# A fused mask-and-maximum, a moved load and a new instruction order in an attention-plus-experts kernel

## The chip, the cores and the metric

The kernel runs on one core of one Trainium2 chip. The core has a matmul engine (TensorE, PE in the profile), three engines for elementwise work (VectorE or DVE, ScalarE or ACT, GpSimd or POOL), and a sync engine (SyncE, SP) that here only issues DMAs. Each engine takes its instructions strictly in the order in which the program has them; semaphores hold an instruction until what it needs is there. The metric is the device time of one execution in microseconds (us), as the median over runs.

## The reference

Two layers follow each other. The first is attention inside clusters: for 4 batches and 8 heads, 768 positions and 64 dimensions per head, q and k are assigned to the nearest of 16 centres, and a position attends only to positions of its own cluster.

```python
q_assign = np.argmax(np.einsum('bhsd,hcd->bhsc', q_n, c_n), axis=-1)
k_assign = np.argmax(np.einsum('bhsd,hcd->bhsc', k_n, c_n), axis=-1)
mask = q_assign[:, :, :, None] == k_assign[:, :, None, :]
scores = np.where(mask, scale * np.matmul(q, k.transpose(0, 1, 3, 2)), -1000000000.0)
attn = softmax(scores);  x = np.matmul(attn, v)
```

The second is a mixture of 4 experts over x (4 x 768 x 512). A gate picks 2 experts per position; each expert is a causal attention head with its own wq, wk, wv (512 x 64) and wo (64 x 512):

```python
scores = scale * (q @ k.transpose(0, 2, 1))
scores = np.where(causal, -1000000000.0, scores)   # causal: key after query
a = softmax(scores);  ye = a @ v @ wo[e];  out += mask * w * ye
```

## The kernel before

The work is cut into 24 pairs. Pairs n = 0 to 15 are two attention heads of one batch each; n = 16 to 23 are two experts of one batch each (the "MoE" pairs, two per batch). A pair goes through these steps:

- *Operands* (`attention_operands`, `moe_operands`). For attention, q and k are loaded, transposed on TensorE (L531), multiplied with the normalised centres (L562), transposed again (L569), and VectorE finds the nearest centre (L574 to L582, L600). A one-hot row of the cluster, times a large number, is appended to q and k, so that a plain matmul gives masked scores. For MoE pairs q and k are projected (L764) and split into a high and a low part.
- *Row maxima* (`core`, from L955 on). L978 gives the scores of 128 queries against a block of keys in a PSUM bank, and VectorE's L988 reduces the bank to its maximum. In MoE pairs the block on the diagonal first gets the causal mask: L986 adds `tri` (128 x 128, 0 or -2^33) to the bank's last 128 columns. With 6 row blocks and 2 heads there are 12 such blocks per MoE pair, of width 128, 256, 384, 512, 320 and 384. L1004 (L1025 in pair 0) transposes the maxima, and a small DMA writes them as one more row of q.
- *Scores and values*. L1059 and L1060 compute the scores again, transposed; ScalarE's L1065 takes the exponential into a tile p; in MoE pairs GpSimd's L1070 clears what lies behind the diagonal; L1103 multiplies with v. The row sums are gathered in `acc` by additions on GpSimd or VectorE (L381, L382) and summed over partitions by L1127. The p tiles come from a ring: more tiles in the first layer, four (p0 to p3) in the MoE pairs, taken in turn, one per key block.
- *Normalising and output*. The sums travel through DRAM to be spread over partitions (`rb`). For MoE pairs VectorE or GpSimd multiplies `avu` by `rb`, one engine copies the high part (into `kt` or `xk`), and another subtraction gives the low part (`qt` or `xq`); `moe_out` (L1213) multiplies with wo, six blocks of 128 positions per batch, copies each from PSUM and stores it.

All of this is written as a list of operations. `plan.op` gives each a number, the engine, and for some an alternative engine. `SEQ`, a list of words, is the order in which they are issued: the word 3047p is operation 3047 on its alternative engine GpSimd (a: ScalarE, d: VectorE), a word without a letter the operation on its first engine. `SLOT` says which of its buffers each tile uses; `ps`, eight PSUM banks, is the longest. Because every engine keeps program order, SEQ fixes the order of all queues.

Constants and the centres' preparation (`centroid_op`) are not in SEQ; they are issued before it. SP loads the centres first (`dma(cf, ...)`), then k and q of pair 0. VectorE makes the constants, then squares the centres (L434), ScalarE takes the square root (L435) and loads the table of Exp by a dummy exponential (L436) that writes column 2 of the small tile `nr`; VectorE's L438 writes the same column. L443 gives the normalised centres, L449 transposes them and L453 copies them. `blk` (L425, L426, L444) and `tri` (L403) are made on the way. 37 `spin` operations (L1229) are matmuls that compute nothing and keep TensorE running in the head.

## Time and profile before

| | us |
|---|---|
| median of 3 runs | 701.16 (699.75 to 703.5) |
| the profiled execution | 701.95 |
| its span in the profile | 700.2 |
| TensorE busy | 680.8 (97%) |
| VectorE busy | 554.7 (79%) |
| ScalarE busy | 350.5 (50%) |
| GpSimd busy | 345.5 (49%) |

The span runs from the first to the last instruction of one execution; the time of that execution is 1.75 us longer. Busy is the time in which an engine executes; waiting for a semaphore is not counted. Mean durations of VectorE's operations are from start to end, and neighbours overlap a little. [...]

### The profile page before, as it was taken

To read this page: it belongs to the slowest core of one execution; us is meant where nothing else is said; L and a number is where in the kernel's file an instruction comes from. 1 tells how busy PE (TensorE), PEld (TensorE's weight loads), DVE (VectorE), ACT (ScalarE), POOL (GpSimd) and SP (SyncE) were. 2 spreads that over 40 slices of the span, in tenths; PEclk is the share of its full clock that TensorE was granted. 3 is DMA by queue.
4 is the path that set the end of the run, shared out by engine and by line. 5 is a ranking of instruction groups with operands and counts; after the bars stand their busy time and mean duration, and the time that the engine had idled before them with its cause. 6 is when DMAs were issued, how large, how long until landed. Compare 5 with 4: busy or idle time off the path is not lost.

```text
span 700.2 us, 13106 instructions
## 1 busy us (share of the span) xinstructions
PE 680.8 (97%) x4523; PEld 526.6 (75%) x4523; DVE 554.7 (79%) x1215; ACT 350.5 (50%) x863; POOL 345.5 (49%) x285
## 2 busy tenths in 40 slices
PE   8999999999999999999999999999999989999997
PEld 6778767767767767767767688879779877877876
DVE  6998798888899688989999977783887766467842
ACT  5447545645645735656746532543452344333653
POOL 4585647479656387575486516134322236242221
PEclk9999999999999999999999999999999999999999
DMA  8766759678665777687859744537455455554223
GB/s 231 197 149 157 182 130 239 145 163 236 174 157 147 190 188 196 164 199 180 172 136 252 172 115 123 152 117 172 107 130 129 100 138 153 124 131 122 87 85 121
DMA packets 78094, 109.64 MB, mean 157 GB/s; under 512 B 22432, under 2 KB 61516, under 8 KB 78028
## 3 DMA queue, kind: packets, MB, share of 16 engines
q1 hardware_dynamic: 78028, 108.81, 62.0%
q8 instruction: 36, 0.59, 0.4%
q14 instruction: 30, 0.25, 0.1%
HBM read 36.54 MB, written 12.91 MB: 71 GB/s over the span
## 4 chain that ended last, share of the span: by engine, by line
PE 81%; DVE 9%; DMA 4%; issue 2%; ACT 1%; POOL 1%; SPq 1%; DVEq 0%; ACTq 0%; POOLq 0%
PE ps L1103 20%; PE ps L978 12%; PE ps L1059 11%; PE ps L1060 11%; PE ps L764 9%; PE ps L1213 5%; PE ps L816 4%; DVE mx L988 3%; PE ps L531 2%; PE ps L1127 2%; DMA tq<-mr 1%; DVE oh L582 1%; PE ps L562 1%; SPq L369 1%; DMA vt<-x 1%
## 5 line engine op out<-in xcount | busy, mean ns | idle before, releaser
L988 DVE TENSOR_REDUCE mx<-ps 128x1 f32<-128x384 f32 (+1 forms) x448 | 223.1, 544 | 24.6 <-PE ps L978 22.5
L1059 PE MATMUL ps<-tq,tk 128*128 128x384 f32 (+2 forms) x528 | 178.4, 341 | 1.2 <-ACT p L1065 1.2
L1060 PE MATMUL ps<-tq,tk 97*128 97x384 f32 (+2 forms) x528 | 173.7, 332 | 1.1 <-DMA tq<-mr 1.0
L1065 ACT ACTIVATE p<-ps 128x384 f32<-128x384 f32 (+2 forms) x288 | 119.2, 461 | 64.8 <-PE ps L1060 39.3
L978 PE MATMUL ps<-tk,tq 80*128 80x384 f32 (+4 forms) x512 | 144.9, 353 | 4.2 <-ACT avu L376 1.9
L1059 PEld LDWEIGHTS ps<-tq,tk 128*128 128x128 f32 x528 | 100.3, 190 | 10.3 <-issue 3.8
L978 PEld LDWEIGHTS ps<-tk,tq 80*128 80x128 f32 x512 | 89.4, 190 | 21.7 <-issue 9.1
L1060 PEld LDWEIGHTS ps<-tq,tk 97*128 97x128 f32 x528 | 100.6, 191 | 2.7 <-DMA tq<-mr 1.8
L381 POOL TENSOR_TENSOR acc<-acc,p 128x768 f32<-128x768 f32 (+2 forms) x37 | 58.2, 1574 | 63.3 <-DVE acc L382 26.2
L1070 POOL TENSOR_SCALAR_AFFINE_SELECT p<-p 128x256 f32<-128x256 f32 x48 | 21.6, 466 | 76.2 <-ACT p L1065 57.1
L1065 ACT ACTIVATE xl<-ps 128x384 f32<-128x384 f32 x88 | 40.7, 497 | 26.3 <-PE ps L1060 26.0
L1103 PE MATMUL ps<-p,vt 128*64 128x384 f32 x288 | 50.7, 491 | 0.0
L986 DVE TENSOR_TENSOR ps<-ps,tri 128x128 f32<-128x128 f32 x96 | 28.1, 292 | 22.4 <-PE ps L978 22.3
L381 POOL TENSOR_TENSOR acc<-p,p 128x768 f32<-128x768 f32 (+1 forms) x11 | 19.3, 1754 | 50.6 <-ACT p L1065 34.0
L376 ACT ACTIVATE hi<-ps 128x384 fp32r<-128x384 f32 x38 | 18.6, 492 | 48.6 <-PE ps L764 38.9
L1103 PE MATMUL ps<-p,vm 128*64 128x384 f32 (+2 forms) x288 | 41.5, 423 | 0.0
L1065 ACT ACTIVATE xh<-ps 128x384 f32<-128x384 f32 x80 | 37.8, 498 | 5.2 <-PE ps L1060 4.7
L382 DVE TENSOR_TENSOR acc<-acc,p 128x768 f32<-128x768 f32 (+2 forms) x33 | 26.8, 811 | 14.8 <-POOL acc L381 7.7
L1103 PEld LDWEIGHTS ps<-p,vt 128*64 128x64 f32 x288 | 19.6, 136 | 23.7 <-issue 21.4
L1178 POOL TENSOR_TENSOR xt<-avu,rb 128x384 f32<-128x384 f32 x26 | 26.6, 1035 | 15.7 <-DMA rb<-rd 15.7
L988 DVE TENSOR_REDUCE M<-ps 128x1 f32<-128x512 f32 (+3 forms) x64 | 31.4, 491 | 2.2
L1103 PEld LDWEIGHTS ps<-p,vm 128*64 128x64 f32 x288 | 18.5, 136 | 19.1 <-issue 13.5
(271 smaller groups left out, 1447.6 us busy)
## 6 DMA issues: line engine op xcount, KB each, us to landing
tq<-hi SPq DMA_DIRECT2D x88, 192.0 KB
tk<-hi SPq DMA_DIRECT2D x60, 192.0 KB
tk<-lo SPq DMA_DIRECT2D x46, 192.0 KB
rb<-rd SPq DMA_DIRECT2D x46, 192.0 KB
tq<-lo SPq DMA_DIRECT2D x45, 192.0 KB
vt<-in_v_dram SPq DMA_DIRECT2D x16, 384.0 KB
x<-xt SPq DMA_DIRECT2D x16, 384.0 KB
tk<-hi SPq DMA_DIRECT2D x16, 384.0 KB
```

Of the source, the lines that this page charges most:

```text
L381: ways = [("pool", t_pool(n), lambda: POOL.tensor_tensor(dst(), a(), b(), op=fn)), ("dve", t_dve(n), lambda: DVE.tensor_tensor(dst(), a(), ...
L382: ("dve", t_dve(n), lambda: DVE.tensor_tensor(dst(), a(), b(), op=fn))]
L764: PE.matmul(m()[:, :HW], w_()[:, dc, es], x_[dc]()[:, c], start=(i == 0), stop=(i == 3 * DC - 1))
L816: PE.matmul(m()[:, :NV], x_[dc]()[:, ts], w_()[:, dc, :], start=(i == 0), stop=(i == 3 * DC - 1))
L978: PE.matmul(ps()[:, :w], Q[0:R, 0, h, c * 128:(c + 1) * 128], K[0:R, 0, h, i * w:(i + 1) * w], start=True, stop=True)
L986: DVE.tensor_tensor(e, e, tri, op=OP.add)
L988: DVE.tensor_reduce(to, ps()[:, :w], axis=AX.X, op=OP.max)
L1059: PE.matmul(p()[:, o_:HW], K[:, 1, h, ks], Q[:, 1, h, qs], start=True, stop=False)
L1060: PE.matmul(p()[:, o_:HW], K[0:R, 0, h, ks], Q[0:R, 0, h, qs], start=False, stop=True)
L1065: ACT.activation(pt()[:, h, o_:HW], p()[:, o_:HW], AF.Exp, scale=SC)
L1103: PE.matmul(av()[h * 64:(h + 1) * 64, o_:HW], d["vv"](h, kc), pt()[:, h, o_:HW], start=(kc == 0), stop=(kc == nk - 1), tile_position=(0, 6 ...
L1213: PE.matmul(m(), a_()[:, ts], w_()[:, ep, :], start=(ep == 0 and i == 0), stop=(ep == EP - 1 and i == 2))
```

## The change

- The centres' load is issued by ScalarE instead of SP.
- The dummy exponential writes a fifth column of `nr`. The small constants are set after the centres are normalised, and the four operations that make `blk` and the mask part of `tri` become one operation in SEQ (`go_blk`, operation 39; all later numbers go up by one). The first two L651 matmuls name it as needed.
- `tri` is 512 wide: 384 columns of 0, then the old 128. On the diagonal block one `tensor_tensor_reduce` adds it to the whole width and gives the maximum; it replaces L986 and L988 there. It writes the sum back to the bank.
- The exponentials of the last, 128 wide key block of a half (`o_ == 256`) go into the first 128 columns of the tile of the block before it, which uses only columns 128 to 383.
- The gate's scratch tiles use the buffers of two attention tiles.
- In the last batch the last of the six output blocks is made in two halves of 256 columns.
- SEQ and SLOT are new as a whole.

```diff
-    dma(cf, centroids.rearrange("h c d -> (h c) d"))
+    ACT.dma_start(cf, centroids.rearrange("h c d -> (h c) d"))
...
-        nr = sb.tile([128, 4], FT, name="nr")
+        nr = sb.tile([128, 5], FT, name="nr")
...
-        ACT.activation(nr[:, 2:3], nr[:, 0:1], AF.Exp, scale=0.0)
+        ACT.activation(nr[:, 4:5], nr[:, 0:1], AF.Exp, scale=0.0)
...
+        DVE.memset(tri[:, :384], 0.0)
...
+    def go_blk():
+        DVE.tensor_scalar(pi, pi, 67, None, op0=OP.bitwise_and)
+        DVE.tensor_scalar(di, di, 6, None, op0=OP.arith_shift_right)
+        DVE.tensor_tensor(blk, pi, di, op=OP.is_equal)
+        DVE.tensor_scalar(tri[:, 384:], jp, 0.0, -BIG, op0=OP.is_gt, op1=OP.mult)
     cbd_ready = centroid_op()
+    blk_ready = op("dve", 1.0, go_blk, base(0) + 10, at=4.9)
...
+                    to = mx()[:, h, cc, i:i + 1] if nb == 2 else tops(h)[:, cc:cc + 1]
                     if moe and i == nb - 1:
-                        e = ps()[:, w - 128:w]
-                        DVE.tensor_tensor(e, e, tri, op=OP.add)
-                    to = mx()[:, h, cc, i:i + 1] if nb == 2 else tops(h)[:, cc:cc + 1]
-                    DVE.tensor_reduce(to, ps()[:, :w], axis=AX.X, op=OP.max)
+                        DVE.tensor_tensor_reduce(ps()[:, :w], ps()[:, :w], tri[:, 512 - w:], 1.0, -3.0e38, OP.add, OP.max, to)
+                    else:
+                        DVE.tensor_reduce(to, ps()[:, :w], axis=AX.X, op=OP.max)
...
+                po = o_ - (256 if o_ == 256 else 0)
+                if po == o_:
+                    pt = p_tile(n)
...
-                        ACT.activation(pt()[:, h, o_:HW], p()[:, o_:HW], AF.Exp, scale=SC)
+                        ACT.activation(pt()[:, h, po:po + w], p()[:, o_:HW], AF.Exp, scale=SC)
...
+        blocks = [(c, 0, DM) for c in range(NC)]
+        if final:
+            blocks[-1:] = [(NC - 1, 0, DM // 2), (NC - 1, DM // 2, DM)]
```

Of SEQ, the two lines of before and of after that hold the operation 3047 (3048 after) and its neighbours:

```diff
-3526 3425 3215 3523 3178 3289 3288 3047p 3435 3297 3528 3304 3412 3216 3048 3312 3306 3433 3428 3120 3309 3307 3446
...
+3430 3428 3288 3048 3447 3523 3297 3306 3528 3524 3448 3527 3216 3179 3529 3289d 3217 3180 3441 3449 3298 3443 3433
```

There 3047 (after: 3048) is the subtraction xq = avu - xk of pair 17, 3215 and 3178 (3216 and 3179) are L1127 of pair 18, and 3288 (3289) is the first addition into `acc` of pair 19.

## Rows read from the trace of the kernel before

**Rows 1.** Windows by stage: length, busy PE, PEld, DVE, ACT, POOL; PEclk, DMA, GB/s.
```profile
28.00:400.00 372.00, 365.24 (x2435) 268.54 (x2434) 330.24 (x671) 215.28 (x513) 236.40 (x159) 1.00 0.73 177
400.00:680.00 280.00, 274.55 (x1810) 227.97 (x1810) 196.78 (x472) 115.34 (x312) 91.86 (x99) 0.99 0.49 126
```

**Rows 2.** Chain that ended last, first 40 us; columns: start, length (us), what.
```profile
0.81 0.39 SPq L369
...
1.26 0.42 SPq L369
...
1.73 4.70 DMA qt<-in_q_dram
...
10.29 0.57 DVE sm L574
...
22.84 2.65 DVE mx L988 x6
...
25.80 0.57 PE ps L1025 x3
```

**Rows 3.** Windows of 2 us at the longest stall; columns as rows 1.
```profile
560.00:562.00 2.00, 0.11 (x2) 0.04 (x1) 1.93 (x4) 0.58 (x2) 1.39 (x1) 1.00 0.98 252
562.00:564.00 2.00, 2.00 (x6) 1.84 (x7) 1.93 (x6) 1.66 (x5) 0.00 (x0) 0.51 0.64 143
564.00:566.00 2.00, 2.00 (x10) 1.62 (x9) 0.66 (x2) 0.49 (x3) 0.00 (x0) 0.64 0.01 3
```

**Rows 4.** Timeline there: start, us, engine, line, operation [idle before <- releaser].
```profile
558.34 1.28 POOL L381 TENSOR_TENSOR acc<-p,p 128x512 f32<-128x512 f32 x1 [6.57 <-PE ps L1127]
...
559.58 1.80 POOL L381 TENSOR_TENSOR xq<-avu,xk 128x768 fp32r<-128x768 f32 x1
...
561.42 0.49 ACT L376 ACTIVATE avu<-ps 128x384 f32<-128x384 f32 x1 [2.72 <-POOL xq L381]
...
561.96 0.65 PE L978 MATMUL ps<-tk,tq 80*128 80x384 f32 x1 [1.89 <-ACT avu L376]
```

**Rows 5.** Timeline of the head, VectorE and ScalarE; columns as in rows 4.
```profile
2.45 0.90 DVE L426 TENSOR_SCALAR acc<-acc 128x256 int32<-128x256 int32 x1
...
3.27 0.21 DVE L434 SCALAR_TENSOR_TENSOR avu<-rb 128x64 f32<-128x64 f32 x1
3.41 0.08 DVE L434 DVE_READ_ACCUMULATOR avu<-rb 128x1 f32 x1
...
3.74 1.28 ACT L436 ACT_TABLE_LOAD   x1
...
5.27 0.16 DVE L438 RECIPROCAL nr<-nr 128x1 f32<-128x1 f32 x1 [1.36 <-ACT nr L436]
...
6.44 0.42 DVE L444 TENSOR_TENSOR blk<-acc,acc 128x256 fp32r<-128x256 int32 x1
```

**Rows 6.** VectorE by form: xcount | busy us, mean ns | idle before.
```profile
L988 DVE TENSOR_REDUCE mx<-ps 128x1 f32<-128x384 f32 x416 | 208.4, 548 | 23.7 <-PE ps L978 22.1
L986 DVE TENSOR_TENSOR ps<-ps,tri 128x128 f32<-128x128 f32 x96 | 28.1, 292 | 22.4 <-PE ps L978 22.3
...
L582 DVE TENSOR_TENSOR oh<-ps,sm 128x384 bf16<-128x384 f32 x16 | 16.4, 1023 | 0.6
...
L575 DVE TENSOR_TENSOR ps<-ps,sm 128x384 f32<-128x384 f32 x16 | 9.1, 567 | 1.2
```

**Rows 7.** TensorE's waits from 400 to 680 us: total us, times, longest.
```profile
PE ps L1059 <- ACT p L1065: 1.2, 1, 1.2
...
PE ps L978 <- ACT p L1065: 0.7, 1, 0.7
```

**Rows 8.** Page, costliest groups: the causal mask on GpSimd; columns as in rows 6.
```profile
L1070 POOL TENSOR_SCALAR_AFFINE_SELECT p<-p 128x256 f32<-128x256 f32 x48 | 21.6, 466 | 76.2 <-ACT p L1065 57.1
```

**Rows 9.** Chain that ended last, its end; columns as in rows 2.
```profile
696.02 0.60 ACT xt L376
```

**Rows 10.** Busy time after the last matmul; columns as in rows 1.
```profile
696.00:698.00 2.00, 0.00 (x0) 0.00 (x0) 0.00 (x0) 0.60 (x1) 0.00 (x0) 1.00 1.01 375
```

## The prediction

> **What bounds the kernel now.** I read the page's busy shares and its chain first, then the busy time by stage, then the chain of the first 40 us, the timelines around the head and around the longest stall, and the tail. The busy shares (table above) put TensorE at 97%. By stage the reader sees that from 28 to 400 us TensorE is busy 365.24 of 372 us, and from 400 to 680 us 274.55 of 280 [rows 1]. So 6.76 + 5.45 = 12.2 us of waiting is left between head and tail, and the matmuls themselves, which the change does not make fewer, are the rest. VectorE is busy 330.24 of 372 us in the first of these stages but only 196.78 of 280 us in the second [rows 1]: work taken from it in the second stage is no work on the path.

> The head is another matter. Until 25.80 us, when the transposes of the first maxima run, the chain goes over the loads of k and q, q's transposes and the cluster matmuls, and then almost without a break over VectorE from 10.29 us on [rows 2]. The reader is to see there that q's load is late because of its place in SP's row of issues, and that from 10.29 us on VectorE's queue is what is long.

> [...] The timeline names the chain: a GpSimd sum into acc waited 6.57 us for L1127's matmuls, the subtraction xq<-avu,xk stood behind it on GpSimd and took 1.80 us, ScalarE's copy into avu waited for that, and L978 waited 1.89 us for the copy to free its PSUM bank [rows 4].

> **The change part by part.** Times are set against the profiled execution, 701.95 us (span 700.2), and moved by 701.95 - 701.16 = 0.79 us to the median at the end.

> *Loads.* The centres' load held SP's first place: SP issued it at 0.81 and k at 1.26 us [rows 2]. On ScalarE's queue it leaves k and q 0.45 us earlier. Bounds: 0, if the DMA engines and not the issue set q's landing, and 0.45; I take 0.45, since the row starts earlier with the same bytes behind it. On ScalarE the new issue is in front of everything; if the first table load stood in front of it, the centres would come 1.28 us later (the length of such a load [rows 5]), and that is covered by the next item.

> *Exp table.* L438 waits 1.36 us for the ScalarE instruction that loads the Exp table, because both write the same column of nr; with a column of its own that wait goes, and the normalised centres come 1.36 us sooner [rows 5]. What is late next is q: its second transpose and copy end after the centres. So little of the 1.36 is on the path. The centres' transposes leave the space between q's two transposes and go behind them; I count nothing for that.

> *Work put behind the centres.* The four index and mask operations (blk, tri) become one planned operation, which the new sequence puts on VectorE after q's second copy and before the first cluster maximum (L574). The longest of its parts takes 0.90 us, blk's comparison 0.42 [rows 5]; with the two others at 0.42 too, a bit over 2 us in all. They begin when q's second copy is done, by estimate at 7.4 us (q's landing at 6.43 - 0.45 = 5.98, then some 1.4 us for transposes and copy), and end near 9.5; a subtraction of 384 columns, priced as L575 at 0.57 [rows 6] less its overlap, follows. L574 could then start at 9.9 against 10.29 us: of the gain of 0.45 about 0.4 stays. Later on this queue the new sequence has one operation of 0.55 less before the first maxima and one of 0.4 more. Together the head gives -0.5 us. Bounds: -1.36 (the whole wait) and +0.5 (no earlier landing, and the planned operation late by its 0.9).

> *Mask and maximum in one.* 96 times (8 pairs, 2 heads, 6 row blocks) L986 (0.292) and L988 (0.548 at 384 columns) become one operation over the whole width [rows 6]. The trace has none of this kind. Nearest is L575, two operands and a PSUM result over 384 columns, 0.567 [rows 6], plus a read of the accumulator as behind L434, 0.08 [rows 5]: 0.65 against 0.84, so -0.19 x 96 = -18 us of VectorE. Bounds: -0.27 x 96 = -26 without the read, and with L582's 1.023 [rows 6] plus the read 1.10, +0.26 x 96 = +25 us. All of this lies in the stage where VectorE has 83.2 us free [rows 1], so I count 0 on the path; the upper end is a rival below.

> *Narrow exponentials share tiles.* Per MoE pair 7 instead of 9 tiles are taken from a ring of four. TensorE's two waits on exponentials in that stage are 1.2 and 0.7 us [rows 7], so 0 to -1.9; against it stands that GpSimd's mask of one key block and ScalarE's exponential of the next now write one tile, twice per pair, and if the one waited for the other each time, 16 x 0.466 = +7.5 [rows 8]. I take 0, since they write different columns.

> *Last block in halves.* The new sequence still ends on a whole block (c = 1), with one half before it. After the last matmul come the same copy of 0.60 [rows 9] and issue; the queue, which moves 375 GB/s from 696 to 698 us, has 128 KB less before it, at most -0.34 us [rows 10]. [...] I take -0.1, bounds -0.35 and +0.1.

> *The new sequence.* It leaves the amount of TensorE work alone. What I can read from it is the place of the chain at 560 us. Before, the subtraction was word 3047p, on GpSimd, right behind that waiting sum. Now it is word 3048, on VectorE, ahead of L1127's two operations, and the sum (3289d) is behind them. The chain cannot come back in that form. The stall goes: 1.89 us, and with it the slow clock, (1 - 0.51) x 2 + (1 - 0.64) x 2 = 1.70 us [rows 3, 4]. That is -3.6 us. The other 12.2 - 1.9 = 10.3 us of waits I leave as they are: the new sequence removes some and makes others. Against it speaks that between the transposes of a pair's maxima and its first scores there are now 8.3 TensorE entries on average instead of 11.1 (counted over 23 pairs in both sequences). Bounds: -5 (half of them go) and +3.6 (a stall with a slow clock somewhere else).

> Sum: 701.95 - 0.5 - 0.1 - 3.6 = 697.75, less 0.79: **697.0 us**.

> **The rivals.** *A stall of the same price comes up elsewhere:* only head and tail are won, 697.0 + 3.6 = 700.6. For it: the shorter cover above, and in-order queues with every engine. Against: only one wait in the stage from 28 to 680 us was long enough for the clock to fall.

> *The short waits go too:* half of 10.3, 697.0 - 5.1 = 691.9. For it: they are many and small, and VectorE gets time back. Against: the cover again.

> *The fused operation is slow, and the kernel gets slower.* At 1.10 us instead of 0.84, twelve of them add 0.26 x 12 = 3.1 us to each MoE pair on VectorE, right before the transposes of its maxima (L1004). VectorE is free only 30% of that stage [rows 1], so between none and 70% of it, 0 to 2.2 us per pair, reaches TensorE; with 1 us per pair, 697.0 + 8 = 705.0. It decides from about 0.84 us on for 384 columns. For it: no operation of this kind is in the trace, and L582 shows that two operands can cost 1.023. Against: L575 reads PSUM and SBUF too and takes 0.567 [rows 6]. [...]

> **How the numbers follow.** Forecast 0.50, same price elsewhere 0.22, short waits go too 0.12, slow fused operation 0.16. The forecast alone has a range of 694.5 to 699.5. The range that holds 8 in 10 reaches from the short-waits rival to between the first rival and the slow one: 691.8 to 702.8. A measurement of this kernel can tell about 0.5%, 3.5 us: faster is below 697.65, slower above 704.67. Faster: 0.32 of the forecast's 0.50, 0.12 of the short waits, 0.02 of the first rival, together 0.46. Slower: half of the slow rival and 0.03 of mishaps in the others, 0.11. The rest, 0.43, is no change.

> **What would show it.** In the changed profile: k's issue at about 0.8 us and q's first transpose near 6.0; no wait of VectorE on the Exp instruction; L574 near 9.9 and the first L1025 near 25.3 us; 96 operations of about 0.65 at 384 columns with VectorE's busy time from 400 to 680 us down by some 18; no two-microsecond hole and no slow clock in the MoE stage; the last matmul about 4 us earlier, and the same 4 us from there to the end. Wrong would be: a fused operation over 0.84, a hole with a slow clock at another place, or TensorE's waits from 28 to 680 us above 12 us.

## The result, and the profile after

The changed kernel took 693.68 us (median of 4 runs, 691.71 to 696.02) against 700.64 us before: a ratio of 0.9895, 95% interval 0.9853 to 0.9937. Timed again beside the experiments it took 692.76 us (6 runs) against 699.54, ratio 0.9897 (0.9863 to 0.9932). It is faster, by about 7 us where 4.2 were forecast (701.16 to 697.0); 697.0 lies 3.3 to 4.2 us too high, and the time is nearer to the rival "the short waits go too" (691.9) than to the forecast. Two executions of it were profiled, one of 696.02 us (span 694.3) and one of 692.21 us (span 690.5).

First the stages [rows 1] of both; PEclk is TensorE's granted clock as a share of the full one, and the number in brackets behind a busy time is how many instructions of the engine fell into the window. The profile of 696.02 us:

```profile
28.00:400.00 372.00, 367.81 (x2455) 270.48 (x2454) 325.63 (x658) 218.58 (x522) 242.41 (x167) 1.00 0.72 177
400.00:680.00 280.00, 276.80 (x1832) 231.21 (x1833) 183.90 (x493) 113.98 (x313) 75.61 (x89) 0.99 0.49 128
```

The profile of 692.21 us:

```profile
28.00:400.00 372.00, 368.98 (x2459) 271.15 (x2458) 326.42 (x660) 218.31 (x522) 243.46 (x169) 1.00 0.71 177
400.00:680.00 280.00, 277.61 (x1858) 231.61 (x1857) 185.62 (x494) 115.44 (x316) 75.13 (x87) 1.00 0.49 129
```

TensorE idles for 4.19 + 3.20 = 7.4 and 3.02 + 2.39 = 5.4 us where it idled for 12.2. The count of matmuls says more. From 28 to 400 us it starts 2455 and 2459 instead of 2435, and from 400 to 680 us 1832 and 1858 instead of 1810, of the same list of matmuls but for six more at the very end. The second stage gains more matmuls than its idle time explains (the 692.21 us profile idles 3.06 us less there and starts 48 more, at some 0.155 us each 7 us). Of the other 4 us, 1.70 are the slow clock of before's profile, by estimate from its 0.51 and 0.64 in two windows of 2 us [rows 3]; matmuls of 384 columns start 0.32 us apart there (562.76 to 563.40 us), against 0.18 before the hole (554.97 to 555.51). The rest is, by the author's estimate, waiting that was counted as busy, as a_two_ops shows it below. Out of the list of waits of the 696.02 us profile, TensorE from 28 to 680 us (total, times, longest):

```profile
PE ps L975 <- DMA tq<-hi: 1.7, 2, 1.4
PE ps L975 <- ACT p L1064: 1.7, 1, 1.7
...
PE ps L1058 <- DVE M L983: 0.9, 1, 0.9
PE ps L590 <- DVE oh L579: 0.5, 2, 0.3
```

The waits on the clustering, 1.9 us at L593 and 1.7 at L607 before, are down to 0.5 at L590 and none. The hole at 560 us is gone [rows 3, 4]. But a hole of the same price stands at 520 us. Windows as in rows 3, and the copy and the wait that make it:

```profile
520.00:522.00 2.00, 0.26 (x5) 0.13 (x1) 0.52 (x1) 1.40 (x3) 0.03 (x1) 1.00 0.08 19
522.00:524.00 2.00, 2.00 (x9) 1.80 (x10) 2.00 (x5) 0.83 (x3) 2.00 (x1) 0.78 0.60 206
524.00:526.00 2.00, 2.00 (x8) 2.00 (x7) 0.46 (x3) 0.49 (x1) 0.12 (x1) 0.50 0.78 191
526.00:528.00 2.00, 2.00 (x12) 2.00 (x11) 1.12 (x2) 0.00 (x0) 0.00 (x0) 0.86 0.04 8
```

```profile
520.60 0.84 ACT L376 ACTIVATE xh<-vt 128x768 fp32r<-128x768 f32 x1 [3.94 <-DMA vt<-x]
521.35 0.85 ACT L1064 ACTIVATE p<-ps 128x384 f32<-128x384 f32 x2
...
521.87 0.51 PE L975 MATMUL ps<-tk,tq 80*128 80x512 f32 x1 [1.74 <-ACT p L1064]
```

ScalarE stands 3.94 us at a copy whose load has not landed, two exponentials stand behind it, and TensorE waits 1.74 us for the PSUM bank that the first of them frees. The granted clock then falls as far as 0.50: here TensorE loses the time of the wait and, by estimate from the clocks 0.78, 0.50 and 0.86 of three windows of 2 us, some 1.7 us more.

The new operation, by form (count, busy us, mean ns), to be set against L986 and L988 of before [rows 6]; its two rows are the operation itself and the read of its maximum:

And the head [rows 2, 5]:

```profile
6.96 0.50 ACT L376 ACTIVATE xq<-ps 128x384 f32<-128x384 f32 x1
7.33 0.40 ACT L450 ACTIVATE cbd<-ps 128x256 f32<-128x256 f32 x1
...
7.78 0.52 PE L559 MATMUL ps<-xq,cbd 128*32 128x384 f32 x2 [1.24 <-ACT cbd L450]
...
9.98 0.55 DVE L571 TENSOR_REDUCE sm<-ps 128x24 f32<-128x384 f32 x1
```

q's transposes begin at 5.23 instead of 6.47 us and no row of VectorE waits for the Exp instruction; yet the first L1022 (L1025 before) is at 26.29 us, 0.49 later than before.

### The profile page after: what moved, and what is told of

Its sections match the earlier page's. It is cut to its first block, busy times and chain, and to the rows that moved or that the text cites. A ratio compares the mean times of both kernels' runs of the same rounds, so it can differ in the third digit from the quotient of the medians.

```text
span 694.3 us, 13123 instructions
## 1 busy us (share of the span) xinstructions
PE 678.3 (98%) x4529; PEld 526.0 (76%) x4529; DVE 537.1 (77%) x1216; ACT 348.4 (50%) x866; POOL 337.0 (49%) x283
## 4 chain that ended last, share of the span: by engine, by line
PE 81%; DVE 6%; DMA 6%; issue 3%; POOL 2%; ACT 2%; SPq 1%; DVEq 0%; ACTq 0%; POOLq 0%
PE ps L1102 18%; PE ps L975 12%; PE ps L1058 12%; PE ps L1059 11%; PE ps L761 10%; PE ps L813 5%; PE ps L1216 4%; PE ps L528 2%; PE ps L1126 2%; DVE mx L985 2%; DMA vt<-x 2%; DMA tq<-hi 1%; PE ps L559 1%; DVE oh L579 1%; PE ps L648 1%
## 5 line engine op out<-in xcount | busy, mean ns | idle before, releaser
L985 DVE TENSOR_REDUCE mx<-ps 128x1 f32<-128x384 f32 (+1 forms) x416 | 209.1, 547 | 29.7 <-PE ps L975 27.2
L975 PE MATMUL ps<-tk,tq 80*128 80x384 f32 (+3 forms) x512 | 146.8, 352 | 5.3 <-DMA tq<-hi 1.7
L1058 PEld LDWEIGHTS ps<-tq,tk 128*128 128x128 f32 x528 | 100.0, 189 | 10.3 <-issue 3.8
L975 PEld LDWEIGHTS ps<-tk,tq 80*128 80x128 f32 x512 | 90.3, 189 | 20.3 <-issue 6.1
L1069 POOL TENSOR_SCALAR_AFFINE_SELECT p<-p 128x256 f32<-128x256 f32 x48 | 20.2, 435 | 102.6 <-ACT p L1064 95.3
L381 POOL TENSOR_TENSOR acc<-acc,p 128x768 f32<-128x768 f32 (+2 forms) x31 | 49.2, 1587 | 40.6 <-DVE acc L382 27.4
L983 DVE CUSTOM_DVE_ANT_0 ps<-ps,tri 128x384 f32<-128x384 f32 (+4 forms) x96 | 47.3, 516 | 23.2 <-PE ps L975 22.2
L1064 ACT ACTIVATE xh<-ps 128x384 f32<-128x384 f32 x80 | 38.6, 498 | 11.9 <-PE ps L1059 11.2
L376 ACT ACTIVATE hi<-ps 128x384 fp32r<-128x384 f32 x45 | 21.9, 494 | 33.2 <-PE ps L761 23.1
L382 DVE TENSOR_TENSOR acc<-acc,p 128x768 f32<-128x768 f32 (+2 forms) x39 | 31.8, 816 | 7.4 <-POOL p L1069 3.9
L381 POOL TENSOR_TENSOR lo<-xk,hi 128x384 fp32r<-128x384 f32 x24 | 24.1, 1015 | 17.7 <-DMA tq<-lo 5.6
L376 ACT ACTIVATE avu<-ps 128x384 f32<-128x384 f32 x27 | 13.0, 488 | 39.1 <-PE ps L1102 35.1
```

The source lines that it names most:

```text
L376: return op("act", t_act(n, sbuf), lambda: ACT.activation(dst(), src(), AF.Copy), due, after, use, alt=("dve", t_dve(n), lambda: DVE.tenso ...
L381: ways = [("pool", t_pool(n), lambda: POOL.tensor_tensor(dst(), a(), b(), op=fn)), ("dve", t_dve(n), lambda: DVE.tensor_tensor(dst(), a(), ...
L382: ("dve", t_dve(n), lambda: DVE.tensor_tensor(dst(), a(), b(), op=fn))]
L975: PE.matmul(ps()[:, :w], Q[0:R, 0, h, c * 128:(c + 1) * 128], K[0:R, 0, h, i * w:(i + 1) * w], start=True, stop=True)
L983: DVE.tensor_tensor_reduce(ps()[:, :w], ps()[:, :w], tri[:, 512 - w:], 1.0, -3.0e38, OP.add, OP.max, to)
L985: DVE.tensor_reduce(to, ps()[:, :w], axis=AX.X, op=OP.max)
```

## The experiments

All were timed in five rounds beside the kernel before, in three groups: the first four, then b_fused to b_share, then the last four. Before's medians there were 699.54, 700.72 and 700.57 us, so kernels of different groups are compared by their ratios to it. The numbers of lines are those of after in kernels that start from after, and of before in the others; where an edit adds lines, its own rows are one to three lines off.

**after_again.** The changed kernel itself.

> The kernel after once more, with another profile. Theory (the gain is the hole at 560 us, its slow clock and some shorter waits; the hole at 520 us that the first profile of after shows hangs on one late landing of 7.89 us of v's load): about 693.5 us, 7 below before; no hole near 560 us; TensorE's waits from 28 to 680 us at or below 7.4 us, and where the hole at 520 us is missing, at about 5.5 and with no slow clock. Rival (the hole at 520 us belongs to the new order, a stall of the same price in another place): it stands in this profile too, with a wait near 1.7 us and granted clocks of 0.5 to 0.8 behind it.

692.76 us. Its profile, the second pair of rows above, has the hole at 520 us again, with a wait of 1.95 us, and behind it the clock stays at 1.00. That is the rival's wait without its slow clock. So the hole belongs to the new order, and the slow clock behind a hole of this length came in the one execution (0.50 behind 1.74 us) and not in the other (1.00 behind 1.95 us).

**a_two_ops.** The fused operation undone, the order kept.

```diff
-    DVE.tensor_tensor_reduce(ps()[:, :w], ps()[:, :w], tri[:, 512 - w:], 1.0, -3.0e38, OP.add, OP.max, to)
+    e = ps()[:, w - 128:w]
+    DVE.tensor_tensor(e, e, tri[:, 384:], op=OP.add)
+    DVE.tensor_reduce(to, ps()[:, :w], axis=AX.X, op=OP.max)
```

> The kernel after with mask and maximum again as two VectorE operations (an addition over 128 columns, then the reduction), its order unchanged. Theory (the fused operation lies beside TensorE's work): 0 to +0.7 us against after, so 693.5 to 694.2; VectorE's busy time from 400 to 680 us back from 183.9 to about 197. Rival (VectorE's relief is what shortened the waits): TensorE's waits from 28 to 680 us go from 7.4 back to 10 or 12 us and the time rises by 3 to 5, to 697 or 698.

700.1 us against 699.54 before (ratio 1.0006, 0.9985 to 1.0027): 7.3 us slower than after, the whole gain. The theory fell. The rival has the sign, but the rise is more than its 3 to 5 us and not where it put it: TensorE idles for 6.7 us from 28 to 680 us, not for 10 to 12. Its stages:

```profile
28.00:400.00 372.00, 368.76 (x2456) 270.38 (x2455) 326.78 (x658) 218.28 (x522) 243.43 (x167) 1.00 0.72 177
400.00:680.00 280.00, 276.56 (x1808) 225.93 (x1807) 203.31 (x487) 113.19 (x311) 74.17 (x88) 1.00 0.48 127
```

Up to 400 us it is like after (2456 matmuls). From there it starts 1808, 50 fewer than after's second profile, although idle time is only 1.05 us longer. The view of one tile shows where. M takes the maxima of the diagonal blocks of up to 512 columns, 64 of the 96 (the others go into mx first). Who waited for M's writers from 400 to 680 us (us, times), with two operations:

```profile
  PEld ps L1058: 2.4, 7
  PEld ps L975: 2.2, 5
...
  PE ps L975: 0.9, 3
  PE ps L1058: 0.5, 1
```

With the fused one, the 692.21 us profile has one such row of TensorE left (the 696.02 us profile has two weight loads, of 1.2 and 0.8 us):

```profile
  PEld ps L975: 0.2, 1
```

The weight loads (PEld: the operand of a matmul that is loaded ahead of it, at 502.97 us for the matmul at 503.14) wait 0.2 to 0.8 us each, 4.6 us in all at these two lines, and the matmuls there only 1.4. For the rest the matmul before is still counted as busy: at 505.41 us a weight load has waited 0.17 us, and its matmul has no wait in the list. What it costs comes out when the two traces are laid side by side, since both kernels issue the same 4529 matmuls in the same order. The matmul that after's second profile starts at 400 us comes 0.9 us later in a_two_ops, the one at 680 us 7.4 us later. Of the 6.5 us between, 5.2 arise in 20 steps, each at a matmul that, or whose weight load, waited for one of VectorE's maxima (4.0 us for M, 1.2 for mx). 2.5 us arise at matmuls for which the trace names no cause, and 1.4 are won back, because the hole at 520 us is only 0.5 us long in a_two_ops.

**a_sub_late.** One word moved back behind the waiting addition.

```diff
-... 3288 3048 3447 ... 3529 3289d 3217 ...
+... 3288 3447 ... 3529 3289d 3048 3217 ...
```

> The kernel after with one word moved: the subtraction xq = avu - xk (3048) stands again behind the first addition into acc (3289), which waits for TensorE. Theory (that chain made the hole): a hole of about 1.9 us comes back near 555 us with a slow clock behind it, +3.6 us against after, so about 697. Rival (the hole came from the old order around it as much as from this chain; the new order gives the copy another bank or more time): 0 to +1 us.

694.85 us, ratio 0.9916 (0.9888 to 0.9945). That is 2.1 above after by the medians, 1.3 by the ratios, and the intervals overlap. No hole came back at 555 us; the longest wait on avu is 0.6 us. Laid beside after's second profile, this one is already 3.1 us behind at 400 us, where the two orders are still the same; the wait on avu adds 0.7, and its shorter hole at 520 us gives 0.9 back. In the new order the chain alone does not make the hole.

**b_swap.** Before, with two words exchanged.

```diff
-... 3289 3288 3047p 3435 ...
+... 3289 3047p 3288 3435 ...
```

> The kernel before with two words exchanged: the subtraction 3047 stands ahead of the waiting addition 3288 on GpSimd, nothing else. Theory: the hole at 560 us goes, 1.9 us of waiting and 1.7 us of slow clock, so -3.6 us, about 697.0. Rival (another wait takes its place, since the addition now comes 1.8 us later): 0 to -1 us, with a hole in the next 20 us.

697.64 us against 699.54, ratio 0.9970 (0.9952 to 0.9988): -1.9 us by the medians, half of the 3.6, between theory and rival. The two-microsecond hole is gone; a wait of 1.0 us at L978 stands at 557 us in its place, so that some 0.9 us of waiting is won. The slow clock has left 560 us as well, but this profile has it at 96.5 us:

```profile
94.00:96.00 2.00, 0.84 (x6) 0.53 (x5) 2.00 (x5) 0.49 (x1) 1.56 (x2) 1.00 0.52 136
96.00:98.00 2.00, 2.00 (x11) 1.90 (x12) 1.55 (x5) 1.63 (x4) 0.96 (x1) 0.63 0.78 188
98.00:100.00 2.00, 2.00 (x10) 1.37 (x10) 0.59 (x2) 0.67 (x2) 0.00 (x0) 0.52 0.37 110
```

There TensorE waits 1.2 us at L607 for VectorE, as it does in before, whose clock stays at 1.00 there. Over all runs the mean granted clock was 0.9988 here and 0.9980 in before; times the span that is a difference of some 0.6 us, by estimate. So the 1.9 us are about 0.9 of waiting and 0.6 of clock, and the rest is not told apart from noise.

**b_fused.** Before, with the fused operation alone (tri is 512 wide, and the gate's scratch tiles have moved to make room).

```diff
-                        e = ps()[:, w - 128:w]
-                        DVE.tensor_tensor(e, e, tri, op=OP.add)
...
+                        DVE.tensor_tensor_reduce(ps()[:, :w], ps()[:, :w], tri[:, 512 - w:], 1.0, -3.0e38, OP.add, OP.max, to)
```

> The kernel before with the fused operation alone (tri 512 wide, the gate's scratch tiles in the buffers of two attention tiles for room), order and everything else as before. By now after with two operations ran at 700.1 against 692.8, so the fused operation is on the path there. Theory A (in short bursts of diagonal blocks VectorE is full whatever the order, and each block costs 0.25 to 0.3 us more with two operations): the old order gains too, 3 to 6 us, so 694 to 697 where before runs at 699.5. Theory B (only the new order, laid out for the short operation, puts TensorE right behind it; the old order keeps its distance): 0 to -1.5 us.

697.96 us against 700.72, ratio 0.9969 (0.9951 to 0.9986): -2.2 us by the ratio, between the two theories. Where they arise is not shown: laid beside the profile of b_share, which has two operations and the same order, this one is 0.6 us ahead at 680 us, and the trace puts no step of that down to a diagonal block. The hole is in its profile as in rows 3, with the full clock behind it:

```profile
560.00:562.00 2.00, 0.10 (x2) 0.04 (x1) 1.97 (x3) 0.58 (x2) 1.39 (x1) 1.00 0.98 252
562.00:564.00 2.00, 2.00 (x10) 1.58 (x11) 1.87 (x7) 1.81 (x5) 0.00 (x0) 1.00 0.63 141
564.00:566.00 2.00, 2.00 (x13) 1.87 (x12) 0.81 (x4) 1.13 (x3) 0.00 (x0) 1.00 0.19 36
```

**b_all.** Before, with the fused operation, the exchange, the centres' load on ScalarE and nr's fifth column.

```diff
-    dma(cf, centroids.rearrange("h c d -> (h c) d"))
+    ACT.dma_start(cf, centroids.rearrange("h c d -> (h c) d"))
...
-        ACT.activation(nr[:, 2:3], nr[:, 0:1], AF.Exp, scale=0.0)
+        ACT.activation(nr[:, 4:5], nr[:, 0:1], AF.Exp, scale=0.0)
```

> The kernel before with the fused operation, the exchange of 3047 and 3288 (-1.9 us alone), the centres' load on ScalarE's queue and the fifth column of nr; the old order otherwise. If the edits add up and the order as a whole is worth little beside them: under Theory A 692 to 695, the level of after (692.8). Under Theory B 696.5 to 698, and the rest of the way to after is the new order's.

697.63 us, ratio 0.9955 (0.9936 to 0.9973), -3.1 us. That is Theory B's range. The edits give 3.1 us together where 1.9 + 2.2 and the head were to be had singly, which the interval does not tell apart, and the remaining 4 us to after need the new order with the fused operation. This profile too has the slow clock at 96 us (0.64 and 0.50) and the full one at 560.

**a_old_ends.** After, with both ends as before.

```diff
-    ACT.dma_start(cf, centroids.rearrange("h c d -> (h c) d"))
+    dma(cf, centroids.rearrange("h c d -> (h c) d"))
...
-        ACT.activation(nr[:, 4:5], nr[:, 0:1], AF.Exp, scale=0.0)
+        ACT.activation(nr[:, 2:3], nr[:, 0:1], AF.Exp, scale=0.0)
...
-            blocks[-1:] = [(NC - 1, 0, DM // 2), (NC - 1, DM // 2, DM)]
```

> The kernel after with both ends as before: centres loaded first on SP, the dummy exponential in nr's third column, the last block whole. Theory (from the traces: head's gain is lost behind the planned operation and GpSimd's memsets, the tail won 0.6): first L1022 at 26.3 to 26.8 us, time 0 to +1.2 us against after. Rival (the head's 1.24 us at q's first transpose is worth all of it): first L1022 near 27.5 us, +1.2 to +1.8 us with the tail.

693.44 us, ratio 0.9902 (0.9880 to 0.9924): no difference to after that can be measured. L571 starts at 10.55 us, 0.57 later than in after, and the first L1022 at 26.43, only 0.14 later. From the end of the last matmul to the end of the span it is 3.70 us, in after 3.68 and in before 4.25: the half blocks give nothing, and the 0.6 us come with the order.

**b_share.** Before, with the shared exponential tiles alone.

```diff
+                po = o_ - (256 if o_ == 256 else 0)
+                if po == o_:
+                    pt = p_tile(n)
-                pt = p_tile(n)
```

> The kernel before with the shared exponential tiles alone: 7 tiles of the ring of four per MoE pair instead of 9. Theory (predicted): 0, at most -0.7 us, 699 to 700. Rival (TensorE's two waits on exponentials, 1.2 and 0.7 us, come from the ring): -1.9 us, 697.6. Second rival (GpSimd's mask and the next exponential wait for each other on one tile): slower by up to 7 us.

701.09 us against 700.72, ratio 1.0004 (0.9987 to 1.0021): nothing, as expected. Tiles of their own under the new order were not tried.

**a_pad.** After, with a VectorE operation more behind each fused one.

```diff
+    junk = consts.tile([128, 1], FT)
...
+                        DVE.tensor_reduce(junk, tri[:, :192], axis=AX.X, op=OP.max)
```

> The kernel after with one more small VectorE operation behind each of the 96 fused ones: a maximum over 192 columns of the constant mask into a spare column, by estimate 0.2 to 0.3 us each, which nothing reads. Theory (it is VectorE's time in the bursts of diagonal blocks that TensorE runs into): nearly what two operations cost, +4 to +7 us against after, and waits of TensorE on L983 and its neighbours again. Rival (what counts is the length of the chain from a block's scores to its maximum and its free bank, which this operation does not lengthen): 0 to +2 us.

694.9 us, ratio 0.9920 (0.9895 to 0.9946): +1.6 us to after by the ratios (2.1 by medians of two groups), although VectorE has as much to do as in a_two_ops, 202.47 us from 400 to 680 us. The rival holds. VectorE's timeline in one burst of diagonal blocks, first with two operations, then with the pad, then after (692.21 us profile; start, us):

```profile
504.48 0.29 DVE L984 TENSOR_TENSOR ps<-ps,tri 128x128 f32<-128x128 f32 x1
504.80 0.56 DVE L985 TENSOR_REDUCE M<-ps 128x1 f32<-128x384 f32 x1
505.27 0.29 DVE L984 TENSOR_TENSOR ps<-ps,tri 128x128 f32<-128x128 f32 x1
```

```profile
502.43 0.56 DVE L984 CUSTOM_DVE_ANT_0 ps<-ps,tri 128x384 f32<-128x384 f32 x1
502.90 0.15 DVE L984 DVE_READ_ACCUMULATOR2_ANT M<- 128x1 f32 x1
502.90 0.35 DVE L985 TENSOR_REDUCE junk<-tri 128x1 f32<-128x192 bf16 x1
503.17 0.56 DVE L984 CUSTOM_DVE_ANT_0 ps<-ps,tri 128x384 f32<-128x384 f32 x1
```

```profile
501.38 0.56 DVE L983 CUSTOM_DVE_ANT_0 ps<-ps,tri 128x384 f32<-128x384 f32 x1 [0.25 <-PE ps L975]
501.86 0.14 DVE L983 DVE_READ_ACCUMULATOR2_ANT M<- 128x1 f32 x1
501.86 0.60 DVE L983 CUSTOM_DVE_ANT_0 ps<-ps,tri 128x384 f32<-128x384 f32 x1
502.38 0.14 DVE L983 DVE_READ_ACCUMULATOR2_ANT M<- 128x1 f32 x1
```

From one block to the next VectorE needs 505.27 - 504.48 = 0.79 us and 503.17 - 502.43 = 0.74 with the pad. After needs 502.38 - 501.86 = 0.52: the read of a block's maximum starts together with the next operation, as at 501.86. The pad takes nearly all of VectorE's saving back, and costs some 2 of the 7.3 us. What it leaves alone is the time from taking a block up to its maximum: 0.88 us with two operations (504.48 to 505.36), and with one 0.66 (501.86 to the end of the read at 502.38) or, beside the pad, 0.62. Laid beside after's second profile like a_two_ops, a_pad falls 4.1 us behind from 400 us on, but of that 1.7 are, by estimate, a slow clock behind the hole at 520 us (a wait of 2.4 us; the granted clock is 0.99 over the stage), and only some 1.0 arise at VectorE's maxima, against 5.2 in a_two_ops. So some 5 us hang on the length of the chain and not on VectorE's time, as far as medians of this spread (about 1.5 us each way) can tell.

**a_xh.** After, with the copy of the hole at 520 us behind two exponentials on ScalarE (and what follows it on VectorE, xl, behind two maxima).

```diff
-... 3041 3380 3378 3177 3186 3381 3193 2923 3119 3255 3258 3189 3190 3042 3385 3268 3191 ...
+... 3041 3378 3177 3186 3193 3380 2923 3119 3255 3258 3189 3190 3042 3268 3381 3385 3191 ...
```

> The kernel after with the one hole near 520 us taken apart: on ScalarE the copy xh<-vt (3380), which waits for v's third load, goes behind the two exponentials 3186 and 3193, and on VectorE xl<-vt,xh (3381) behind two maxima (3258, 3268). Theory: the wait of 1.7 to 1.95 us at L975 goes, the first nine of L761's twelve matmuls cover the copy: -1.5 to -2 us, and no slow clock there, 690 to 691.5. Rival (L761 then waits for the same landing): 0.

693.13 us, ratio 0.9898 (0.9874 to 0.9921): unchanged. The wait at L975 went, and this one came:

```profile
PE ps L761 <- ACT gr L859: 1.3, 1, 1.3
```

The rival's kind of outcome: the next late thing on ScalarE's queue, now the small copy gr behind the moved one, holds TensorE in its turn.

**a_blk.** After, with two parts of the planned operation back in VectorE's wait for the centres.

```diff
-        DVE.tensor_scalar(pi, pi, 67, None, op0=OP.bitwise_and)
-        DVE.tensor_scalar(di, di, 6, None, op0=OP.arith_shift_right)
```

(in `go_blk`; the same two lines stand ahead of `blk`'s tile instead)

> The kernel after with two of the planned operation's four parts (the and and the shift, 0.87 and 0.90 us there) put back where before had them, into VectorE's 1.46 us of waiting for the centres' load. Theory (they stand on the head's chain in after): L571 at 8.8 to 9.3 instead of 9.98 us, first L1022 near 25.4 instead of 26.3, time -0.5 to -0.9 us. Rival (the centres' copy cbd on ScalarE, for which L559 waits, or GpSimd's memsets before 26 us are what is late): first L1022 at 26.0 to 26.3, time unchanged.

692.62 us, ratio 0.9893 (0.9870 to 0.9915): unchanged, and the first maximum of the clustering starts when it did:

```profile
10.00 0.56 DVE L573 TENSOR_REDUCE sm<-ps 128x24 f32<-128x384 f32 x1 [1.41 <-PE ps L568]
```

VectorE now waits 1.41 us there. So the planned operation was not the last on the chain; the copy cbd on ScalarE (in after at 7.33 us, behind the copies of k and q), L559 and the copy s are.

**a_best.** Both edits together.

```diff
-... 3041 3380 3378 3177 3186 3381 3193 ...
+... 3041 3378 3177 3186 3193 3380 2923 ...
```

> The kernel after with both edits of a_xh and a_blk. If both theories hold, they add up: -2 to -3 us against after, 690 or a little below, with no hole over 1.5 us between 28 and 680 us. If only the hole's holds, about 691.

692.46 us, ratio 0.9881 (0.9858 to 0.9904): the lowest median, and not to be told from after's 0.9897. Its profile has no wait over 0.8 us between 28 and 680 us, and still the 690 to 691 us that were expected without the hole did not come: taking the last long hole out of the new order gave nothing that these runs can measure.

## Why the prediction was right in sign and wrong in its reasons

*Mask and maximum in one: the step that failed.* "All of this lies in the stage where VectorE has 83.2 us free, so I count 0 on the path." The duration was about right: 0.573 us at 384 columns with the read of 0.142 beside the next block, against 0.65 predicted, and VectorE's busy time differs by 203.31 - 185.62 = 17.7 us between a_two_ops and after, against 18 predicted (against before it fell by only 11.2 us, since the new order puts other work on VectorE in that stage: 203.31 us in a_two_ops against 196.78). At the same 384 columns its 573 ns lie beside L575's 567 and not L582's 1023 [rows 6]; what sets those two apart no run shows. But the place was wrong. Taken away from the new order it costs 7.3 us (a_two_ops); put alone into the old one it gives 2.2 (b_fused). The 83 us are an average. The diagonal blocks come in bursts in which VectorE goes from one to the next without a break, and there TensorE's next weight load waits for a maximum to free its bank: 5.2 of the 6.5 us that a_two_ops loses from 400 us on arise at such waits, and a_pad shows that the length from block to maximum counts, more than VectorE's time. In the old order, also with two operations, TensorE keeps a distance to these maxima. The rows of the same view (who waited for M's writers, 400 to 680 us) of before:

```profile
  PEld ps L1004: 0.9, 1
  PE ps L1004: 0.7, 1
  PEld ps L978: 0.6, 1
  PEld ps L816: 0.6, 1
```

That is three weight loads where a_two_ops has twelve at two lines alone. The new order runs close behind the maxima, which the short operation allows.

*The hole at 560 us, -3.6: mis-sized, and it did not come alone.* Removing it in the old order gave 1.9 us (b_swap). The term took 1.89 us of wait and 1.70 of clock as won in full. Of the wait 1.0 came back at L978, and the clock does not hang on this hole alone: behind 1.9 us of idle TensorE it fell to 0.51 in before and stayed at 1.00 in b_fused; behind 1.74 us it fell to 0.50 in after's first profile, and behind 1.95 us it stayed at 1.00 in its second; and in b_swap (0.52) and b_all (0.50) it fell at 96 us instead, in b_swap behind a wait of 1.2 us that before has too, with a clock of 1.00. So "only one wait in the stage from 28 to 680 us was long enough for the clock to fall" read one execution as a rule. And the rival "a stall of the same price comes up elsewhere" is true of the mechanism: the hole at 520 us is in both profiles of after. In waiting, the new order traded one hole for another; what it won lies beside them.

*"The other 10.3 us of waits I leave as they are": wrong.* Without the hole at 520 us the waits from 28 to 680 us are 5.7 and 3.5 us. From 28 to 400 us, where no fused operation is, the new order starts 20 matmuls more, with a_two_ops too (2456): some 3 us by 0.153 us each, mostly the waits on the clustering. Those 3 us are the order's own; they vary between executions, and a_sub_late's profile, with the same order up to there, has only 2441. From 400 us on the same order with two operations loses them again. So the order, with all other edits, is worth nothing without the fused operation (ratio 1.0006), the fused operation without the order 2.2 us, and both together 7.

*The head, -0.5: 0.5 later instead, the upper bound.* k's issue (0.81 us), the Exp wait and L571 (9.98 against 9.9 predicted) came as said, and q's transposes even 1.24 us earlier than in before. What failed is the stretch after L571: 16.31 us to the first L1022, in before 15.51, where 0.15 less was expected; VectorE waits 0.72 us for L648 in it and 0.53 us before L990, which the profile puts down to a GpSimd memset (L465). The edits of the loads and of Exp are worth 0.57 us at L571 (a_old_ends) and 0.14 at L1022: in a_old_ends the first L1022 follows L571 by 15.88 us instead of 16.31, so the time won is waited away there. The planned operation took 2.97 us (6.54 to 9.51 in the second profile) instead of a bit over 2, and that too was covered (a_blk).

*The tail, -0.1: -0.6,* with whole blocks as well. The upper bound of +0.1 rests on no row, and no run shows that half-wide matmuls cost more: in after they start 0.117 us apart (685.28 to 685.63 us) and the whole ones 0.230 (685.63 to 687.01), so two of them take about as long as one. *The shared tiles, 0: right* (b_share).

So 697.0 came from a hole that was priced at twice its worth, and the larger half of the gain, the fused operation in an order made for it, stood in the sum at zero. The forecast's own range, 694.5 to 699.5, misses the 693.68; that the wide range holds it is the rival's doing (short waits, 691.9) and, as to the reasons, luck. One of the prediction's own signs of being wrong came as well: a hole with a slow clock at another place. What stays open: whether the 5 us behind a_pad are the length of the block's chain alone, since two operations also write the bank once more by an instruction of their own; where b_fused's 2.2 us arise; and why the clock falls behind a wait of 1.2 or 1.9 us in one execution and not in the next.

## What to carry to other kernels

Spare time of an engine over a stage says nothing of the bursts in it: before an edit is priced at zero, look at the engine's timeline where its work comes in a row, and ask who needs the result's bank next. The fused operation and the order around it were worth more together (7 us) than apart (2.2 us and none), so time such an edit in both orders. And a matmul engine that is busy for 99% of a stage of 280 us, as in a_two_ops, can still lose over 5 us there at waits of its matmuls and weight loads: count the matmuls per stage, not the idle time.

## What the runs showed of the hardware

- Short waits of TensorE hardly show in its idle time: from 400 to 680 us a_two_ops falls 6.5 us behind after's second profile, matmul by matmul, while its idle time there is only 1.05 us longer (3.44 us).
- A drop of the granted clock to 0.51 and then 0.64 cost 1.70 us in before, by estimate from windows of 2 us, and such drops came behind waits of different length: 1.9 us in before, 1.2 in b_swap. The clock stayed at 1.00 behind the 1.9 us in b_fused and behind the 1.2 us in before.
- The same comparison over 256 columns took 0.42 us in before [rows 5], 0.41 in a_blk beside a GpSimd memset, and 1.18 in after beside a GpSimd subtraction.
- The reading of the fused operation's maximum (0.142 us) started with the next operation and took almost no time of its own: at 384 columns VectorE's next instruction started 0.48 us behind an operation without a reading beside it (501.38 to 501.86) and 0.52 behind one with it (501.86 to 502.38).
